# A fused attention and mixture-of-experts kernel: expert weights fetched in 256 KB pieces, the row-turning steps interleaved, and the first output bank fixed

## The chip, the cores and the metric

The kernel runs on one core of a Trainium2 chip. The metric is device time in microseconds for one execution, the median of several runs. A core has five engines that each run their own instruction list in order and wait for one another through semaphores: TensorE (PE, matrix products, with its weight loads shown apart as PEld), VectorE (DVE), ScalarE (ACT), GpSimd (POOL) and SyncE (SP, which here only issues transfers). POOL issues the indirect transfers (gathers and scatter-adds of rows), SP all others. The transfers run on 16 DMA engines that all queues share.

## What is computed

Windowed attention over 8 batches, 8 heads, 576 positions and 64 channels gives 4608 rows of 512 channels. A gate picks two of eight experts for each row, and each expert is two products with a ReLU between:

```python
logits = x @ w_gate
noise_scale = np.log1p(np.exp(x @ w_noise))
noisy_logits = logits + noise_scale * noise
top2 = np.argpartition(-noisy_logits, 2, axis=1)[:, :2]
...
for e in range(E):                      # 8 experts, w1[e] 512x1024, w2[e] 1024x512
    for k in range(2):
        mask = top2[:, k] == e
        h = np.maximum(x[mask] @ w1[e], 0.0)
        out[mask] += top2_w[mask, k, None] * (h @ w2[e])
```

## The kernel before

Attention and routing take the first quarter of the time and are not touched. Then the experts run one after another, and each expert's rows in chunks (`work`, L644): three chunks for expert 0, and two, of 576 and of 640 rows, for each of experts 1 to 7. The loop at L1116 writes, for each chunk, first `up` (the first product) and then `down` (the second). In both, matrix products are yielded step by step, and `spread` (L77) puts side work between the steps: a part `(a, b, list)` gives its items evenly from share a to share b of the steps. This fixes where an instruction stands in its engine's list; when it runs is set by its waits.

Operands of the products are split in a high and a low part (an ACT copy to `fp32r`, then a DVE subtraction), and every product is three matmuls. `up` for experts 1 to 7 uses seven half-size block products instead of eight (`PRODUCT`, L53); so the rows' planes (`turn`) and the blocks of w1 (`split_w1`) are combined by sums and differences first.

What one chunk needs:

- **Rows.** POOL gathers 128 rows at a time into `xg` (L675); SP writes them to DRAM (`turn_out`, L687, tile `xs`) and reads them back in four transfers in another order (`turn_in`, L692, tile `xc`). All of this for the next chunk stands in the first 0.65 of the steps of `up`.
- **Turning.** `turn` (L719) makes from `xc` the planes of the next chunk, as side work of `down` from step 12.5 to 0.86 of the steps. For each of its five tiles of 128 rows (the last one of a 576-row chunk has 64) there are two items. Item `f` (L728) does two DVE transposes into `tq`, planes 0 to 3 (L737). Item `g` (L745) does, in this order: ACT copy of planes 1 to 3 to `xh` (L749); DVE difference for planes 4 and 5 (L750); DVE low part of planes 1 to 3 (L751); two DVE differences for planes 6 and 7 (L752, L753); ACT copy of planes 4 to 7 (L755); DVE low part of those (L756). `tq` has one buffer, taken anew for each tile.
- **Weights.** One staging tile `ws` of 2 MB holds w1 or w2 of an expert in turn. `load_w1` of the next expert stands at the start of the first chunk's `down`, `load_w2` of the next expert behind the last chunk's `down`, each as a single transfer of 2 MB. `split_w2` stands in 0.55 to 1.0 of the first chunk's `up` and reads `ws` in slices in the order 0, 4, 1, 5, 2, 6, 3, 7; `split_w1` stands in the second chunk's `up` and `down` (its last items up to 0.9 of `down`).
- **Banks.** PSUM has three banks for `up` sums (`ps_z`), one `ps_v` and one `ps_y`. `down` writes its tiles in turn to `ps_d0`, `ps_d1` and `ps_y` (`ring("d")`, L818, a counter that runs on over all chunks), and each is evicted by ACT L997, or for a half tile by ACT L999 and DVE L1000 and L1001. The first product of the next `up` goes to `ps_v`, the second to `ps_y` (`start`, L875).

`down` of experts 1 to 7 begins with 4 steps of its first tile, then two products left over from `up` (`late`) with more steps of tiles 0 and 1 between, and only then the last two slices of w2 (slices 3 and 7, in the entry `(0, 6, 8)` of L967).

Of the kernel before, what the change touches and what calls it, by code (L numbers as in the profile page):

```python
# [8 lines left out]
F32 = mybir.dt.float32  # L9
# [9 lines left out]
N, DM, E, F = 4608, 512, 8, 1024  # L19
# [3 lines left out]
KD, KF = DM // 128, F // 128  # L23
# [7 lines left out]
HALF = WIDE // 2  # L31
# [28 lines left out]
def tiles(e, c):  # L60
    n = chunks(e)[c]
    return [(q, min(128, n - q * 128)) for q in range(-(-n // 128))]
# [25 lines left out]
def tile_kernel(ctx, tc, qT, kT, vx, vT, wgx, noise, w1, w2, out):  # L88
# [123 lines left out]
    def load_w1(e, ks=slice(0, KD), fs=slice(0, F)):  # L212
        if e < E:
            nc.sync.dma_start(w1s[:, ks, fs], w1[e][:, ks, fs])

    def load_w2(e, ks=slice(0, KF)):
        if e < E:
            nc.sync.dma_start(w2s[:, ks], w2[e][:, ks])
# [56 lines left out]
    def split_w2():  # L275
        return lag([(w2s[:, f], W2["h"][:, f], W2["l"][:, f]) for f in (0, 4, 1, 5, 2, 6, 3, 7)])
# [442 lines left out]
    def turn(e, c):  # L719
        if e == 0:  # L720
            return turn_first(c)
        todo = {}

        def begin():
            todo["h"] = XH[e, c] = exa.tile([128, 7, 2, HALF], F32R, name="xh")
            todo["l"] = XL[e, c] = exa.tile([128, 7, 2, HALF], F32R, name="xl")

        def f(q, m):  # L728
            if q == 0:
                begin()  # L730
            w = m // 2
            t = todo[q] = EXB["p"].tile([128, 4 * HALF], F32, name="tq", bufs=1)
            v = t[:, :16 * w].rearrange("p (s x) -> p s x", s=8)
            for h in range(2):
                d = v[:, 2 - 2 * h:4 - 2 * h].rearrange("p s (k x) -> p (s k) x", k=2).rearrange("p k (t c) -> p t k c", c=32)
                a = h * (CHUNKS[c] // 64) + 2 * q
                nc.vector.transpose(d, XC[e, c][:, a:a + w // 32].rearrange("p t (k c) -> p t k c", c=32))  # L737

        def parts(q, m, s0, s1):
            w = m // 2  # L740
            a = todo[q][:, s0 * 2 * w:s1 * 2 * w].rearrange("p (a x) -> p a x", x=w)
            return (a, *(x.rearrange("p a k x -> p (a k) x")[:, 2 * s0 - 2:2 * s1 - 2, q * 64:q * 64 + w]
                         for x in (todo["h"], todo["l"])))

        def g(q, m):  # L745
            w = m // 2
            v = todo[q][:, :16 * w].rearrange("p (s x) -> p s x", s=8)
            a, h, l = parts(q, m, 1, 4)
            nc.scalar.activation(h, a, AF.Copy)  # L749
            nc.vector.tensor_tensor(v[:, 4:6], v[:, 0:1].to_broadcast([128, 2, 2 * w]), v[:, 1:3], op=OP.subtract)  # L750
            nc.vector.tensor_tensor(l, a, h.bitcast(F32), op=OP.subtract)  # L751
            nc.vector.tensor_tensor(v[:, 6], v[:, 1], v[:, 5], op=OP.subtract)  # L752
            nc.vector.tensor_tensor(v[:, 7], v[:, 3], v[:, 6], op=OP.subtract)  # L753
            a2, h2, l2 = parts(q, m, 4, 8)
            nc.scalar.activation(h2, a2, AF.Copy)  # L755
            nc.vector.tensor_tensor(l2, a2, h2.bitcast(F32), op=OP.subtract)  # L756
        return [lambda q=q, m=m, x=x: x(q, m) for q, m in tiles(e, c) for x in (f, g)]

    pair = []

# [13 lines left out]
    EXB, BANKS = {}, {}  # L774
# [41 lines left out]
    late, turns = [], {"z": 0, "d": 0}  # L816
# [141 lines left out]
    def down(e, c):  # L958
        if e == 0:
            yield from down_first(c)  # L960
            return
        wt = GW[e, c]
        hb = HH.pop((e, c))
        w2h, w2l = W2["h"], W2["l"]
        order = (0, 4, 1, 5, 2, 6, 3, 7)
        size = dict(tiles(e, c))
        steps = [(0, 0, 4), None, (0, 4, 6), (1, 0, 2), None, (1, 2, 6), (0, 6, 8), (1, 6, 8)]  # L967
        steps += [(q, 0, 8) for q in size if q > 1]
        P_ = {}
        for s in steps:  # L970
            if not s:
                yield from late.pop(0)
                continue
            q, i0, i1 = s
            m = size[q]
            if i0 == 0:
                P_[q] = ring("d")
            p = P_[q]
            for i in range(i0, i1):
                f = order[i]  # L980
                a, b = dict(start=(i == 0), stop=False), dict(start=False, stop=(i == KF - 1))
                if m == 128:
                    h, l = (hb[:, x, f, q * 128:q * 128 + 128] for x in range(2))
                    nc.tensor.matmul(p, lhsT=h, rhs=w2h[:, f, :], **a)  # L984
                    nc.tensor.matmul(p, lhsT=h, rhs=w2l[:, f, :], start=False, stop=False)  # L985
                    nc.tensor.matmul(p, lhsT=l, rhs=w2h[:, f, :], **b)  # L986
                else:
                    t = hb[:, 0, f, q * 128:q * 128 + 2 * m]
                    nc.tensor.matmul(p, lhsT=t, rhs=w2h[:, f, :], **a)
                    nc.tensor.matmul(p, lhsT=t, rhs=w2l[:, f, :], **b)  # L990
                if i < KF - 1:
                    yield
            if i1 < KF:
                continue
            y = exa.tile([128, XW], F32, name="xg", bufs=XB)[:, :DM]
            if m == 128:
                nc.scalar.activation(y, p, AF.Copy, scale=wt[:, q:q + 1])  # L997
            else:
                nc.scalar.activation(y[:m], p[m:2 * m], AF.Copy)  # L999
                nc.vector.tensor_tensor(y[:m], y[:m], p[:m], op=OP.add)  # L1000
                nc.vector.tensor_scalar(y[:m], y[:m], wt[:m, q:q + 1], None, op0=OP.mult)  # L1001
            add_rows(e, c, q, m, y)
            yield
# [46 lines left out]
    for j in range(NT + 3):  # L1050
# [18 lines left out]
        if W1G // 2 - 4 <= j < W1G // 2 + 4:  # L1069
            k = j - W1G // 2 + 4  # L1070
# [45 lines left out]
    for n, (e, c) in enumerate(work):  # L1116
        nxt = work[n + 1] if n + 1 < len(work) else None
        last = c == len(chunks(e)) - 1
        side, parts = [], []
        if n == 0:  # L1120
            for w in split_w2():
                side += [lambda: (drain(3), drain_slots(1))] * 2 + [w]

            def catch_up():
                while (0, 1, 2) not in XG:
                    drain(1)
                    drain_slots(1)
        elif n == 1:
            pending.append(count())
            side += [lambda: (drain(6), drain_slots(1))] * 12  # L1130
            side += [settle, lambda: drain_slots(10 ** 6), lambda: [x() for x in first_list(2)], lambda: None]
        elif c == 0:
            parts.append((0.55, 1.0, split_w2()))
        if nxt and n:
            rows_of = gather(*nxt)
            if n < 2:
                side += rows_of + [lambda: None] * 2
            else:
                parts.append((0.0, 0.65, rows_of))
        if last and nxt:  # L1140
            nextw = split_w1(e == 0)
            parts += ([(0.55, 0.75, nextw[0]), (0.8, 1.0, nextw[1])] if e else
                      [(a, b, nextw[q]) for q, a, b in ((0, 0.02, 0.12), (1, 0.14, 0.3), (2, 0.33, 0.5), (4, 0.34, 0.5),
                                                       (3, 0.55, 0.75), (5, 0.56, 0.75), (6, 0.8, 1.0))])
        parts.append((0.0, 1.0, side))
        if n == 0:
            parts.append((0.0, 0.8, [zero_out] * ZUP))
        spread(up(e, c) if n else up00, 52 if e else KF * KD - (0 if n else len(taken)), *parts)
        side = turn(*nxt) if nxt else []
        total = KF * len(tiles(e, c)) + (4 if e else 0)  # L1150
        free = 12.5 / total
        if e == 0:
            parts = [(0.7, 1.0, side) if nxt[0] == 0 else (0.05, 0.85, side)]
            if last:
                parts.append((0.0, 0.4, nextw[7]))
        else:
            if c == 0:
                load_w1(e + 1)
            parts = [(free, 0.86, side)]
            if last and nxt:  # L1160
                parts.append((free, 0.9, nextw[2] + nextw[3]))
        if n == 1:
            load_w1(1)
            parts.append((0.0, 0.6, list(other_lists())))
        if n == 0:
            parts.append((0.0, 1.0, [lambda: (drain(3), drain_slots(1))] * 29))
            parts.append((0.68, 0.69, [catch_up]))
            parts.append((0.0, 0.6, [zero_out] * len(blank)))
        spread(down(e, c), total, *parts)
        if last:  # L1170
            load_w2(e + 1)
    ex.close()


# [115 lines left out]
```

## Time and profile before

| what | value |
|---|---|
| median of 3 runs | 1079.51 us (1073.28, 1079.51, 1079.69) |
| span of the profiled execution, first to last instruction | 1070.0 us |
| PE busy | 994.8 us, 93% of the span |
| DVE, ACT, POOL busy | 715.2, 521.8, 338.5 us |
| matmuls of `up` for experts 1 to 7, chunk of 320 columns, one | 310 ns modelled duration |
| matmuls of `down`, 512 columns, one | 390 ns modelled duration |
| `up` of experts 1 to 7 begins | 330 us, then about every 52 us |

The span is 9.5 us under the median and 3.3 us under the fastest run. In the profile a matmul's start is exact enough to see when PE was held up; its end is modelled, and matmuls overlap, so PE's busy share says little about pace. Rows of the list of waits name the waiting engine and line, then who released it, then total us, how many times, and the longest one. In the order of time a number in brackets behind a row is the engine's idle time before it and who ended it.

### The profile page before, as it was taken

Reading aid. Unit: us, or ns where it says so; the run is one execution under the profiler, and the core shown is the slowest. Engines: PE = TensorE matmul, PEld = TensorE weight load, DVE = VectorE, ACT = ScalarE, POOL = GpSimd, SP = SyncE. Lnnn points to the kernel's source line nnn. Section 1 sums busy time; section 2 is a strip of 40 time slices with the busy share of each in tenths; the row PEclk is TensorE's granted clock in tenths of the full one; section 3 lists DMA queues with packets and bytes.
Section 4 is the critical chain, followed back from the end, with each engine's and each line's share of the span. In section 5 each row is a group of like instructions: output and inputs, shape, how many; then the busy total and the mean of one; then the engine's idle time right before and its main releaser. Section 6 shows DMA issues by size and latency. Waiting matters only on the chain.

```text
span 1070.0 us, 22034 instructions
## 1 busy us (share of the span) xinstructions
PE 994.8 (93%) x8433; PEld 882.8 (83%) x8433; DVE 715.2 (67%) x1804; ACT 521.8 (49%) x1305; POOL 338.5 (32%) x465
## 2 busy tenths in 40 slices
PE   8787878779999999999999999999999999999995
PEld 8676767668788898889898889898889897989894
DVE  5688888684276667666776677677666866686630
ACT  4885666432244444544463446354644554454430
POOL 5436636333223141413132213222322323132202
PEclk9998998989999999999999999999999999999998
DMA  9987887874357653665377626762765385537303
GB/s 340 364 259 230 252 257 239 273 230 113 49 131 193 168 115 65 188 169 119 61 204 162 149 25 206 162 145 30 230 136 140 43 244 124 125 69 209 45 2 51
DMA packets 107235, 168.94 MB, mean 158 GB/s; under 512 B 13360, under 2 KB 57648, under 8 KB 105328
## 3 DMA queue, kind: packets, MB, share of 16 engines
q1 hardware_dynamic: 89968, 126.96, 38.7%
q0 software_dynamic: 17152, 40.48, 20.8%
q8 instruction: 68, 1.11, 0.4%
q14 instruction: 47, 0.39, 0.1%
HBM read 110.08 MB, written 57.32 MB: 156 GB/s over the span
## 4 chain that ended last, share of the span: by engine, by line
PE 42%; DVE 30%; ACT 8%; DMA 8%; issue 8%; POOL 1%; SPq 1%; DVEq 0%; POOLq 0%; ACTq 0%
PE ps_z L841 4%; PE ps_z L843 4%; PE ps_z L842 4%; DVE tq L737 4%; DVE WL L234 3%; ACT xh L755 3%; DVE xl L756 3%; DMA xc<-xs 3%; DVE xl L751 2%; PE ps_d L985 2%; PE ps_d L984 2%; PE ps_d L986 2%; DVE ws L264 2%; DVE pt L358 2%; DMA xs<-xg 2%
## 5 line engine op out<-in xcount | busy, mean ns | idle before, releaser
L919 POOL DMA_INDIRECT out_dram<-xg,los x70 | 111.1, 1587 | 423.7 <-ACT xg L997 364.5
L853 ACT ACTIVATE hb<-tq 128x288 fp32r<-128x288 f32 (+1 forms) x168 | 77.1, 459 | 144.4 <-DVE tq L872 138.7
L841 PE MATMUL ps_z<-xh,WH 128*128 128x288 f32 (+1 forms) x448 | 137.4, 307 | 0.9
L842 PE MATMUL ps_z<-xl,WH 128*128 128x288 f32 (+1 forms) x448 | 135.6, 303 | 0.0
L843 PE MATMUL ps_z<-xh,WL 128*128 128x288 f32 (+1 forms) x448 | 135.6, 303 | 0.0
L872 DVE TENSOR_TENSOR tq<-ps_z,tq 128x288 f32<-128x288 f32 (+1 forms) x168 | 79.3, 472 | 81.8 <-PE ps_z L843 76.4
L985 PE MATMUL ps_d<-w2l,hb 128*128 128x512 f32 x328 | 127.9, 390 | 0.0
L984 PE MATMUL ps_d<-w2h,hb 128*128 128x512 f32 x328 | 127.8, 390 | 0.0
L986 PE MATMUL ps_d<-w2h,hb 128*128 128x512 f32 x328 | 127.7, 389 | 0.0
L857 DVE SCALAR_TENSOR_TENSOR hb<-tq,hb 128x320 fp32r<-128x320 f32 (+2 forms) x168 | 75.5, 449 | 37.6 <-ACT hb L853 34.2
L675 POOL DMA_INDIRECT xg<-xrows,lxs x70 | 71.1, 1016 | 83.7 <-DMA xs<-xg 39.0
L841 PEld LDWEIGHTS ps_z<-xh,WH 128*128 128x128 f32 x448 | 84.8, 189 | 5.2 <-DVE tq L872 3.8
L842 PEld LDWEIGHTS ps_z<-xl,WH 128*128 128x128 f32 x448 | 84.8, 189 | 1.1
L755 ACT ACTIVATE xh<-tq 128x512 fp32r<-128x512 f32 (+1 forms) x70 | 42.7, 611 | 87.9 <-DVE tq L753 87.9
L843 PEld LDWEIGHTS ps_z<-xh,WL 128*128 128x128 f32 x448 | 84.7, 189 | 0.0
L756 DVE TENSOR_TENSOR xl<-tq,xh 128x512 fp32r<-128x512 f32 (+1 forms) x70 | 46.6, 666 | 47.4 <-ACT xh L755 47.4
L395 ACT ACTIVATE x<-ps_o,r 128x80 f32<-128x80 f32 x288 | 67.0, 348 | 15.2 <-DVE r L387 15.0
L986 PEld LDWEIGHTS ps_d<-w2h,hb 128*128 128x128 f32 x328 | 61.6, 188 | 13.0
L984 PEld LDWEIGHTS ps_d<-w2h,hb 128*128 128x128 f32 x328 | 61.6, 188 | 12.1
L985 PEld LDWEIGHTS ps_d<-w2l,hb 128*128 128x128 f32 x328 | 61.6, 188 | 11.8
L234 DVE TENSOR_TENSOR WL<-ws,WH 128x512 fp32r<-128x512 f32 x112 | 66.5, 613 | 3.8 <-ACT WH L242 3.4
L749 ACT ACTIVATE xh<-tq 128x384 fp32r<-128x384 f32 (+1 forms) x70 | 35.6, 508 | 68.0 <-DVE tq L737 68.0
(248 smaller groups left out, 2562.5 us busy)
## 6 DMA issues: line engine op xcount, KB each, us to landing
ws<-in_w_dram SPq DMA_DIRECT2D x14, 2048.0 KB
xs<-xg SPq DMA_DIRECT2D x63, 256.0 KB
vw<-in_vx_dram SPq DMA_DIRECT2D x36, 272.0 KB
out_dram<-zero SPq DMA_DIRECT2D x38, 256.0 KB
qc<-in_qT_dram SPq DMA_DIRECT2D x36, 256.0 KB
KW<-in_kT_dram SPq DMA_DIRECT2D x36, 256.0 KB
vt<-in_vT_dram SPq DMA_DIRECT2D x36, 256.0 KB
xrows<-x SPq DMA_DIRECT2D x36, 256.0 KB
```

What stands on the lines that cost most here:

```text
L234: eng.tensor_tensor(l, x, h.bitcast(F32), op=OP.subtract)
L756: nc.vector.tensor_tensor(l2, a2, h2.bitcast(F32), op=OP.subtract)
L841: nc.tensor.matmul(p[:, :n], lhsT=WH[:, a, k, w], rhs=xh[:, b, k, :n], start=first and k == 0, stop=False, **free)
L842: nc.tensor.matmul(p[:, :n], lhsT=WH[:, a, k, w], rhs=xl[:, b, k, :n], start=False, stop=False, **free)
L843: nc.tensor.matmul(p[:, :n], lhsT=WL[:, a, k, w], rhs=xh[:, b, k, :n], start=False, stop=(k == 1), **free)
L853: nc.scalar.activation(hh[:, f, a:b], src, AF.Relu)
L857: nc.vector.scalar_tensor_tensor(hl[:, f, a:m], src[:, :m - a], 0.0, hh[:, f, a:m].bitcast(F32), op0=OP.max, op1=OP.subtract)
L872: nc.vector.tensor_tensor(t, a[:, :n], t, op=OP.add)
L919: s = nc.gpsimd.indirect_dma_start(out=out[:(2 + seen.get((e, c), NT)) * 128], out_offset=bass.IndirectOffsetOnAxis(ap=LT[e, c][1][q][:m], ...
L984: nc.tensor.matmul(p, lhsT=h, rhs=w2h[:, f, :], **a)
L985: nc.tensor.matmul(p, lhsT=h, rhs=w2l[:, f, :], start=False, stop=False)
L986: nc.tensor.matmul(p, lhsT=l, rhs=w2h[:, f, :], **b)
```

## The change

Three edits, all for experts 1 to 7.

1. `turn` takes one `tq` for a whole chunk, and its items change: the second half of `g` (copy and low part of planes 4 to 7) becomes an item `last`, and the list is f0, then for each tile g, the next tile's f, and `last`: 15 items where there were 10, in the same stretch of `down`.
2. `down` sets the bank counter, so that its tiles always go to `ps_d0`, `ps_d1`, `ps_y`, `ps_d0`, `ps_d1`.
3. `load_w2(e)` moves from behind the last `down` of expert e-1 into 0.05 to 0.55 of the first `up` of expert e, as eight transfers of one slice in the order in which `split_w2` reads them. `load_w1(e + 1)` becomes eight transfers in 0.1 to 0.6 of the first chunk's `down`.

```diff
         def f(q, m):
             if q == 0:
                 begin()
+                todo["t"] = EXB["p"].tile([128, 4 * HALF], F32, name="tq", bufs=1)
             w = m // 2
-            t = todo[q] = EXB["p"].tile([128, 4 * HALF], F32, name="tq", bufs=1)
+            t = todo["t"]
...
             nc.vector.tensor_tensor(v[:, 7], v[:, 3], v[:, 6], op=OP.subtract)
+
+        def last(q, m):
             a2, h2, l2 = parts(q, m, 4, 8)
             nc.scalar.activation(h2, a2, AF.Copy)
             nc.vector.tensor_tensor(l2, a2, h2.bitcast(F32), op=OP.subtract)
-        return [lambda q=q, m=m, x=x: x(q, m) for q, m in tiles(e, c) for x in (f, g)]
+        todo_list = tiles(e, c)
+        out_ = [lambda: f(*todo_list[0])]
+        for i, (q, m) in enumerate(todo_list):
+            out_.append(lambda q=q, m=m: g(q, m))
+            if i + 1 < len(todo_list):
+                out_.append(lambda i=i: f(*todo_list[i + 1]))
+            out_.append(lambda q=q, m=m: last(q, m))
+        return out_
...
         P_ = {}
+        turns["d"] = 2
         for s in steps:
...
         elif c == 0:
+            parts.append((0.05, 0.55, [lambda f=f: load_w2(e, slice(f, f + 1)) for f in (0, 4, 1, 5, 2, 6, 3, 7)]))
             parts.append((0.55, 1.0, split_w2()))
...
         else:
+            parts = [(free, 0.86, side)]
             if c == 0:
-                load_w1(e + 1)
-            parts = [(free, 0.86, side)]
+                parts.append((0.1, 0.6, [lambda k=k, x=x: load_w1(e + 1, slice(k, k + 1), slice(x * F // 2, x * F // 2 + F // 2))
+                                         for x in range(2) for k in range(KD)]))
...
         spread(down(e, c), total, *parts)
-        if last:
-            load_w2(e + 1)
```

The line numbers behind the edits grow by up to 11 (L737 becomes L738, L756 becomes L759, L841 becomes L851, L986 becomes L997).

DVE's list in `down` of a first chunk, from the first tile of `turn` to the transposes of the second. Before:

```order
L737 STREAM_TRANSPOSE tq<-xc 128x2x4x32 x2
L750 TENSOR_TENSOR tq<-tq 128x256
L751 TENSOR_TENSOR xl<-tq,xh 128x6x64
L752 TENSOR_TENSOR tq<-tq 128x128
L753 TENSOR_TENSOR tq<-tq 128x128
L756 TENSOR_TENSOR xl<-tq,xh 128x8x64
L737 STREAM_TRANSPOSE tq<-xc 128x2x4x32 x2
```

And of the change, the same place:

```order
L738 STREAM_TRANSPOSE tq<-xc 128x2x4x32 x2
L751 TENSOR_TENSOR tq<-tq 128x256
L752 TENSOR_TENSOR xl<-tq,xh 128x6x64
L753 TENSOR_TENSOR tq<-tq 128x128
L754 TENSOR_TENSOR tq<-tq 128x128
L738 STREAM_TRANSPOSE tq<-xc 128x2x4x32 x2
L759 TENSOR_TENSOR xl<-tq,xh 128x8x64
```

The second tile's transposes now stand between the differences and the low part of planes 4 to 7, which waits for an ACT copy.

PE's list at the border from the second chunk of expert 1 to the first of expert 2: the end of the last tile of `down`, then the first two products of `up`. Before:

```order
L985 MATMUL ps_y_3972<-w2l,hb 128x512
L986 MATMUL ps_y_3972<-w2h,hb 128x512
L841 MATMUL ps_v_3971<-xh,WH 128x288
L842 MATMUL ps_v_3971<-xl,WH 128x288
L843 MATMUL ps_v_3971<-xh,WL 128x288
L841 MATMUL ps_v_3971<-xh,WH 128x288
L842 MATMUL ps_v_3971<-xl,WH 128x288
L843 MATMUL ps_v_3971<-xh,WL 128x288
L841 MATMUL ps_y_3972<-xh,WH 128x288
```

And of the change, at the same border:

```order
L996 MATMUL ps_d_3967<-w2l,hb 128x512
L997 MATMUL ps_d_3967<-w2h,hb 128x512
L851 MATMUL ps_v_3971<-xh,WH 128x288
L852 MATMUL ps_v_3971<-xl,WH 128x288
L853 MATMUL ps_v_3971<-xh,WL 128x288
L851 MATMUL ps_v_3971<-xh,WH 128x288
L852 MATMUL ps_v_3971<-xl,WH 128x288
L853 MATMUL ps_v_3971<-xh,WL 128x288
L851 MATMUL ps_y_3972<-xh,WH 128x288
```

Where the last tile of `down` stood in `ps_y` (4 of the 13 borders with an `up` of experts 1 to 7 behind a `down` of the same), it now stands in `ps_d1`, at every border.

SP's list over one first chunk's `up` and the start of its `down` (`ws` is the staging tile; the transfers `xs` and `xc` in front are those of the chunk before). Before:

```order
L687 DMA xs<-xg 64x512
L692 DMA xc<-xs 32x18x128 x4
L218 DMA ws<-in_w_dram 128x4096
L687 DMA xs<-xg 128x512 x5
L692 DMA xc<-xs 32x20x128 x4
L214 DMA ws<-in_w_dram 128x4096
```

And of the change:

```order
L692 DMA xc<-xs 32x18x128 x4
L218 DMA ws<-in_w_dram 128x512 x2
L687 DMA xs<-xg 128x512 x2
L218 DMA ws<-in_w_dram 128x512
L687 DMA xs<-xg 128x512 x2
L218 DMA ws<-in_w_dram 128x512 x3
L687 DMA xs<-xg 128x512
L218 DMA ws<-in_w_dram 128x512
L692 DMA xc<-xs 32x20x128
L218 DMA ws<-in_w_dram 128x512
L692 DMA xc<-xs 32x20x128 x3
L214 DMA ws<-in_w_dram 128x512 x8
```

Two pieces of w2 stand ahead of the first write of rows, the seventh behind the fifth write, and the eighth behind the first read in the new order.

## Rows read from the trace of the kernel before

**Rows 1.** Waits of PE from 320 us on: total us, times, longest.
```profile
PE ps_y L841 <- DVE xg L1000: 3.2, 2, 1.6
PE ps_y L841 <- ACT xg L997: 3.1, 2, 1.5
PE ps_v L841 <- ACT xh L749: 2.1, 1, 2.1
PE ps_v L842 <- DVE xl L751: 1.8, 8, 0.3
```

**Rows 2.** The same of PE's weight loads.
```profile
PEld ps_v L841 <- ACT xh L749: 5.7, 9, 2.5
PEld ps_v L842 <- DVE xl L751: 4.0, 9, 0.5
PEld ps_y L842 <- DVE xl L756: 2.2, 6, 0.5
```

**Rows 3.** PE in order of time, first `up` of expert 2: start us, us, instruction.
```profile
434.76 0.40 PE L841 MATMUL ps_v<-xh,WH 128*128 128x288 f32 x1
435.41 0.40 PE L842 MATMUL ps_v<-xl,WH 128*128 128x288 f32 x1 [0.25 <-DVE xl L751]
```

**Rows 4.** PE by stretches: us, PE busy (matmuls), granted clock, DMA share, GB/s.
```profile
438.10:441.50 3.40, 3.40 (x16) 0.50 0.83 224
441.50:444.90 3.40, 3.40 (x27) 1.00 0.95 365
...
591.70:595.10 3.40, 3.27 (x12) 0.50 0.20 22
...
332.30:335.70 3.40, 3.37 (x13) 0.50 0.57 77
```

**Rows 5.** The page, part 5: busy us, mean ns, idle us before and its releaser.
```profile
L756 DVE TENSOR_TENSOR xl<-tq,xh 128x512 fp32r<-128x512 f32 (+1 forms) x70 | 46.6, 666 | 47.4 <-ACT xh L755 47.4
```

**Rows 6.** DVE in order of time, first `down` of expert 3.
```profile
569.29 0.46 DVE L857 SCALAR_TENSOR_TENSOR hb<-ps_z,hb 128x288 fp32r<-128x288 f32 x1 [2.47 <-ACT hb L853]
571.78 0.77 DVE L737 STREAM_TRANSPOSE tq<-xc 128x256 f32<-128x256 f32 x2 [2.04 <-DMA xc<-xs]
...
590.42 0.69 DVE L756 TENSOR_TENSOR xl<-tq,xh 128x512 fp32r<-128x512 f32 x1 [0.70 <-ACT xh L755]
```

**Rows 7.** All engines in order of time, the border behind that `down`.
```profile
588.66 0.41 PE L841 MATMUL ps_v<-xh,WH 128*128 128x320 f32 x1
...
590.42 0.59 ACT L999 ACTIVATE xg<-ps_y 64x512 f32<-64x512 f32 x1
```

**Rows 8.** The same at the border from expert 3 to expert 4.
```profile
645.24 0.40 PE L841 MATMUL ps_v<-xh,WH 128*128 128x288 f32 x1
...
645.48 0.35 DVE L751 TENSOR_TENSOR xl<-tq,xh 128x192 fp32r<-128x192 f32 x1
```

**Rows 9.** SP's transfers in order of time, expert 3, both chunks.
```profile
543.09 0.35 SPq L218 DMA_DIRECT2D ws<-in_w_dram  x1
553.46 7.38 SPq L687 DMA_DIRECT2D xs<-xg  x5
562.66 1.97 SPq L692 DMA_DIRECT2D xc<-xs  x4
...
597.66 8.53 SPq L687 DMA_DIRECT2D xs<-xg  x5
```

**Rows 10.** POOL's first gather of each of these chunks.
```profile
544.79 1.02 POOL L675 DMA_INDIRECT xg<-xrows,lxs  x1 [0.30 <-issue]
...
594.31 1.02 POOL L675 DMA_INDIRECT xg<-xrows,lxs  x1 [0.30 <-issue]
```

**Rows 11.** The chain that ended last, 562 to 573 us: start us, us, what.
```profile
564.12 7.44 DMA xc<-xs
```

**Rows 12.** ACT and PE in order of time: last split of w2, first use of its last slices.
```profile
560.55 0.62 ACT L242 ACTIVATE w2h<-ws 128x512 fp32r<-128x512 f32 x1
...
571.38 0.39 PE L984 MATMUL ps_d<-w2h,hb 128*128 128x512 f32 x1
```

More of the change, by code (lines that the diff above doesn't have):

```diff
@@ L740, in parts @@
             w = m // 2
-            a = todo[q][:, s0 * 2 * w:s1 * 2 * w].rearrange("p (a x) -> p a x", x=w)
+            a = todo["t"][:, s0 * 2 * w:s1 * 2 * w].rearrange("p (a x) -> p a x", x=w)
             return (a, *(x.rearrange("p a k x -> p (a k) x")[:, 2 * s0 - 2:2 * s1 - 2, q * 64:q * 64 + w]
@@ L746, in g @@
             w = m // 2
-            v = todo[q][:, :16 * w].rearrange("p (s x) -> p s x", s=8)
+            v = todo["t"][:, :16 * w].rearrange("p (s x) -> p s x", s=8)
             a, h, l = parts(q, m, 1, 4)
```

## Prediction

> **What bounds the kernel now.** I read the page first: PE is busy nearly throughout the expert stage, so the change can win only where PE is held up there. Then I asked for the waits of PE alone, from 320 us on, where experts 1 to 7 run. The reader is to see two kinds [rows 1]. Four waits of about 1.6 us, 3.2 + 3.1 = 6.3 us in all, stand before `ps_y` L841: the second product of an `up` waits until the last tile of the `down` before it is evicted from the same bank (L997, or L999 to L1001). And PE waits for `turn`: once 2.1 us, and eight times up to 0.3 us, for the planes of `xh` and `xl` that its first product reads. The weight loads, which run a step ahead, show the same waits larger, because a modelled matmul end covers part of a hold-up [rows 2]. The order of time shows one: 0.65 us between two matmul starts [rows 3], where 27 of these matmuls take 3.4 us, so 0.13 us each [rows 4].
>
> Next I looked at the granted clock. Three times in this stage it falls to half (1.2 instead of 2.4 GHz) for 3.4 us [rows 4], and each time PE had just waited 1.5 us or more: behind the wait at the first `up` of expert 1, and behind two of the four `ps_y` waits. The other two had no fall behind them.
>
> Last, the order of time of DVE and ACT before a border says why the waits are there. In the first `down` of expert 3, DVE goes through the five tiles of `turn` without a break from 571.78 to 591.11 us, 3.87 us a tile, and in every full tile it stands idle 0.70 us before L756, for the ACT copy of planes 4 to 7 [rows 6]; in the whole kernel that idle time is 47.4 us [rows 5]. PE's next `up` begins at 588.66, while the turning is in its last tile, and the eviction of the last bank (ACT L999, at 590.42) stands behind the turning's copies [rows 7]. At the border to expert 4 it is the same: PE begins at 645.24, and the low part that it needs is made from 645.48 to 645.83 [rows 8].
>
> **The bank order.** The tile in `ps_y` becomes the third of five, evicted in mid `down`, and the last tile lies in `ps_d1`, which no product of `up` writes. The four waits go: 6.3 us [rows 1]. Nothing is added. The next user of `ps_d0` or `ps_d1` is a whole `up` later, and within a `down` a bank comes back after three tiles, as before. Alone this would win a little less, since at these borders the second product would then wait for L756, which ends 0.7 us ahead of the half tile's eviction; with the turning shortened it doesn't.
>
> **The turning.** The same instructions run, in another order: the next tile's two transposes (0.77 us together [rows 6]) now stand where DVE waited 0.70 us for ACT. I count the wait as gone: 2.8 us less before the last tile's L751. At the border of rows 8 that low part ends at 643.0 instead of 645.8, 2.2 us ahead of PE. At the border of rows 7 the last tile's L751 ends at 589.2 now, and 586.4 then, 2.3 us ahead. So these waits go whole. Their size: from below 2.1 + 1.8 = 3.9 us [rows 1]; from above 5.7 + 4.0 + 2.2 = 11.9 us [rows 2]. Start to start, the hold-up of rows 3 is 0.65 - 0.13 = 0.52 us; nine such (the count in rows 2) are 4.7 us; with the 2.2 us for L756 and the 2.1 us at expert 1 that is 9.0. I take 8, leaving 1 us for borders that are not quite cleared. A copy of planes 4 to 7 now stands a little later on ACT, for the last tile behind the eviction of the fourth; the product that reads those planes is PE's second, so about 0.9 us are in hand there beside the 2 us above.
>
> **The clock.** A fall costs (27 - 16) matmuls of 0.13 us, 1.4 us, and at most half of 3.4, 1.7 us [rows 4]. Three cost 4.2 to 5.1 us, if all go because no wait of 1.5 us is left, and nothing is won if other falls come in their place. I take 3.5.
>
> **The weights.** By itself I cost this edit at nothing. What it moves: the first gather of expert 3's second chunk is issued at 544.79, and its first write to `xs` at 553.46, 8.7 us later, while the 2 MB issued at 543.09 are on their way; in the other `up`, without such a load, it is 594.31 to 597.66, 3.4 us [rows 9, 10]. With two pieces, a quarter of the bytes, ahead of the first write, I estimate 3.4 + 5.3 / 4 = 4.7 us, so writes and reads come 4 us earlier, and `xc`, which lands at 571.56 now [rows 11], before 568. DVE reaches its first transposes at 569.75 and waits 2.04 us for `xc` [rows 6]; that wait goes too. But with the shorter turning those 2 us only add to the 2.3 us in hand. SP issues 13 loads as 104, 91 more of about 0.35 us [rows 9], 2.8 us a load on an engine that mostly waits. w1 has slack: its first reader stands in the second `up`, a whole `down` later. w2 is closer: its eighth piece stands on SP behind the first read into `xc`, which waits for all five writes. ACT reaches the split of that slice at 560.55, and PE first needs the last slices at 571.38 [rows 12]. ACT's copy is 0.62 us; DVE's low part and the results of `up` queued behind both I put at 3.7 us. So PE waits only if the piece lands after 567.1. I expect its issue near 559 and its landing before 563.
>
> A page speaks against small transfers. The Trainium skill, "DMA: Bandwidth & Descriptors", section "Anatomy of one DMA — SWDGE (gpsimd) path", gives each transfer about 2.0 us of fixed cost and the bytes at 436 GB/s on top; by that a 256 KB piece is 2.6 us (an estimate, from a path that SP does not use), and eight in a row are 20.8 us, against 6.8 us for one of 2 MB. Started at 543.1 they would end at 563.9, still ahead of 567.1, so the sum by the page is the same. The rows give no price of such a piece in this stage.
>
> **The sum.** 6.3 + 8 + 3.5 = 17.8 us off the span of 1070.0: 1052.2. The median of the runs is 9.5 us over the profiled span, so I forecast 1062. With the bounds of the terms (10.2 to 23.3 us) that is 1056 to 1069.
>
> **Rivals.**
>
> *Banks only (14 in 100).* The ACT copies of the turning wait for PE through the evictions between them, and DVE waits at L756's new place as long as before. For it: the last copy does stand behind the fourth tile's eviction. Against it: DVE trails PE now, so those evictions are due when ACT comes to them. It leaves 6.3 us and two falls of the clock (2.8) less some 2 us for L756 at those borders: 7 us off, 1072.
>
> *Given back (10 in 100).* PE comes earlier to other waits: DVE still has w1's splits to do when `up` begins, and `ps_z` waits for its additions. Against it: DVE's own stretch shrinks by as much as PE comes earlier, and those splits move up with it. At half the gain that is 9 us off: 1071.
>
> *The last piece of w2 comes late (12 in 100), the other side.* The place is the SP queue: the eighth piece is issued behind the first read into `xc`, at worst at 562.7 as now [rows 9], and shares the DMA engines with the reads, which take 7.44 us [rows 11]; landing at 570.4, it holds PE for 570.4 - 567.1 = 3.3 us in each of seven experts, 23 us. That ends at 1062 + 23 = 1085. It decides from a landing after 567.1; at 569.6 (2.5 us an expert) the gain is eaten up, and over 1% slower needs 571.1. Against it: the first writes should come 4 us earlier, not later.
>
> *The pieces are not spread (no chance of its own).* SP is held by waits alone, not by PE's steps, so several pieces may leave together. The time is that of the forecast, because the edit is costed at nothing.
>
> **How the numbers follow.** The forecast has 64 in 100, with its own range of 1056 to 1069. The range for 8 in 10 goes up to the two rivals with a small gain and a little below the forecast's low end: 1055 to 1075. About 1% is what a measurement of this kernel can tell from no change; faster by that means under 1068.7. The forecast lies there but for its edge: 0.64 with a little of the two small-gain cases. Slower by over 1% needs the late piece at its worst, 0.05. The rest, 0.31, is within 1%.
>
> **What would show it.** Right: no wait of PE on L997, L999 or L1000 (new L1008 to L1011) before `ps_y`; the idle time before the low part of planes 4 to 7 (L759) near zero instead of 47.4 us; PE's waits on L751 and L756 (new L752, L759) under 2 us in all; no half-clock stretch from 330 us to the end of the matmuls; the first write of rows in a first chunk's `up` about 5 us behind its gather. Wrong: a PE wait of several us at the entry `(0, 6, 8)` behind w2's split (then the late piece), or ACT waiting for `ws` before L242; DVE idle before L759 as before (banks only); longer waits at `ps_z` (given back); or a span that shrinks without the median following.

## The result: 1% slower, and the profile after

The change takes 1088.07 us (median of 4 runs, 1085.58 to 1095.72), the kernel before 1077.54 us in the same comparison: a ratio of 1.010 with a 95% interval of 1.006 to 1.014. The forecast was 1062, with a range of 1055 to 1075. The profiled execution took 1085.58 us with a span of 1083.9, 13.9 us over the span before. Those two numbers lie 1.7 us apart: the 9.5 us that the forecast put between a span and a median were mostly the spread of the runs. One execution among the experiments below, of the kernel with turning and banks alone, took 1112.84 us at a mean granted clock of 0.84 where the others had 0.975 to 0.979; that kernel's time is the median of the other three.

The waits of PE from 320 us on, to be read against [rows 1]. Columns: total us, times, longest.

```profile
PE ps_z L851 <- DVE tq L882: 16.7, 7, 3.9
PE ps_v L851 <- ACT tq L877: 10.7, 8, 2.5
```

Every wait of [rows 1] is gone: none on the eviction of a `down` tile, none on the turning. In their place stand 27.4 us of waits: 10.7 us inside `up` for evictions of `ps_v`, and 16.7 us for the additions on DVE that empty `ps_z`, all but 0.2 us of it before the products left over from `up` that stand early in `down`. The other engines' waits in the same stretch say where these come from:

```profile
ACT w2h L242 <- DMA ws<-in_w_dram: 40.7, 21, 3.4
DVE w2l L234 <- ACT w2h L242: 37.5, 20, 3.3
```

ACT waits 21 times, two to four times in each of seven experts, for a piece of w2 (some 32 of the 40.7 us for the seventh and the eighth), and DVE, which makes the low part, waits behind it. The order of time of all engines shows one such place, at the first product left over from the first `up` of expert 3:

```profile
568.74 0.63 ACT L242 ACTIVATE w2h<-ws 128x512 fp32r<-128x512 f32 x1 [2.73 <-DMA ws<-in_w_dram]
569.27 0.39 ACT L877 ACTIVATE tq<-ps_v 128x288 f32<-128x288 f32 x1
569.40 0.69 DVE L234 TENSOR_TENSOR w2l<-ws,w2h 128x512 fp32r<-128x512 f32 x1 [2.56 <-ACT w2h L242]
570.01 0.45 DVE L882 TENSOR_TENSOR tq<-ps_z,tq 128x288 f32<-128x288 f32 x1
...
570.52 0.61 PE L851 MATMUL ps_z<-xh,WH 128*128 128x288 f32 x1 [2.91 <-DVE tq L882]
```

The reader is to see one late piece hold two lists. On ACT the split waits 2.73 us for it, and the eviction of `ps_v` stands behind the split. On DVE the low part waits 2.56 us for the split, and the addition that empties `ps_z` stands behind the low part; it starts at 570.01, when the eviction has been over for 0.35 us, so here DVE's own list held it last. PE needs the `ps_z` bank. PE is not waiting for w2.

Why the piece is late is in the chain of what ended last, followed in order of time (start us, us, what):

```profile
542.21 2.91 DMA ws<-in_w_dram
545.20 4.97 DMA xg<-xrows,lxs
550.19 3.97 DMA xs<-xg
554.20 0.70 issue
554.90 6.64 DMA xg<-xrows,lxs
561.56 2.19 DMA xs<-xg
563.83 0.33 SPq L692
564.20 4.52 DMA ws<-in_w_dram
568.74 0.64 ACT w2h L242
```

The first pieces leave at 542.21, and the eighth at 564.20. Between them SP stands in its list at the fifth write of rows (561.56), which waits for the fifth gather. POOL can issue that one only at 554.90, when a buffer of `xg` is written out, and it takes 6.64 us to land. The gather shares the DMA engines with three pieces that SP sent off just before:

```profile
554.25 1.42 SPq L218 DMA_DIRECT2D ws<-in_w_dram  x3
561.56 0.33 SPq L687 DMA_DIRECT2D xs<-xg  x1
561.93 0.43 SPq L218 DMA_DIRECT2D ws<-in_w_dram  x1
563.83 0.33 SPq L692 DMA_DIRECT2D xc<-xs  x1
564.20 0.51 SPq L218 DMA_DIRECT2D ws<-in_w_dram  x1
```

The clock falls too. Two of the stretches at half clock, as in [rows 4] (us, PE busy and matmuls, granted clock, DMA share, GB/s), and the one behind them at nearly full clock:

```profile
461.00:464.40 3.40, 1.56 (x6) 0.50 1.20 196
464.40:467.80 3.40, 3.40 (x10) 0.50 1.07 290
467.80:471.20 3.40, 3.40 (x19) 0.99 0.91 336
```

From 330 us to the end of the matmuls there are eight stretches of 3.4 us at half clock, in six experts; before there were three. The expert stage, from the start of the first matmul of expert 1's `up` to the start of the last matmul, took 726.2 us before and takes 743.5 now.

### The profile page after: what moved, and what is told of

Read it like the earlier page. It is cut to its first block, busy times and chain, and to the rows that moved or that the text cites. A ratio compares the mean times of both kernels' runs of the same rounds, so it can differ in the third digit from the quotient of the medians.

```text
span 1083.9 us, 22236 instructions
## 1 busy us (share of the span) xinstructions
PE 992.7 (92%) x8433; PEld 884.9 (82%) x8433; DVE 712.1 (66%) x1804; ACT 524.2 (48%) x1305; POOL 337.2 (31%) x465
## 4 chain that ended last, share of the span: by engine, by line
PE 42%; DVE 21%; DMA 17%; issue 12%; ACT 4%; POOL 3%; SPq 1%; POOLq 0%; ACTq 0%; DVEq 0%
DMA xg<-xrows,lxs 6%; PE ps_d L995 6%; PE ps_d L996 6%; PE ps_d L997 6%; DMA xs<-xg 5%; DMA ws<-in_w_dram 4%; PE ps_z L851 3%; DVE WL L234 3%; PE ps_z L853 3%; PE ps_z L852 3%; DVE pt L358 2%; DVE xl L759 2%; PE ps_o L376 2%; DVE t L335 1%; DVE mx L340 1%
## 5 line engine op out<-in xcount | busy, mean ns | idle before, releaser
L995 PE MATMUL ps_d<-w2h,hb 128*128 128x512 f32 x392 | 156.4, 399 | 0.0
L851 PE MATMUL ps_z<-xh,WH 128*128 128x288 f32 (+1 forms) x448 | 139.7, 312 | 17.6 <-DVE tq L882 16.7
L996 PE MATMUL ps_d<-w2l,hb 128*128 128x512 f32 x392 | 155.7, 397 | 0.0
L997 PE MATMUL ps_d<-w2h,hb 128*128 128x512 f32 x392 | 155.0, 395 | 0.0
L851 PEld LDWEIGHTS ps_z<-xh,WH 128*128 128x128 f32 x448 | 85.3, 190 | 24.8 <-DVE tq L882 23.2
L997 PEld LDWEIGHTS ps_d<-w2h,hb 128*128 128x128 f32 x392 | 75.3, 192 | 16.4
L995 PEld LDWEIGHTS ps_d<-w2h,hb 128*128 128x128 f32 x392 | 75.9, 194 | 14.8
L996 PEld LDWEIGHTS ps_d<-w2l,hb 128*128 128x128 f32 x392 | 75.8, 193 | 14.3
L851 PE MATMUL ps_v<-xh,WH 128*128 128x288 f32 (+1 forms) x196 | 59.9, 306 | 10.7 <-ACT tq L877 10.7
L234 DVE TENSOR_TENSOR w2l<-ws,w2h 128x512 fp32r<-128x512 f32 x64 | 43.8, 686 | 37.6 <-ACT w2h L242 37.5
L376 PE MATMUL ps_o<-vw,pt 64*64 64x85 f32 x2176 | 54.5, 249 | 13.2 <-issue 6.5
```

What stands on the lines that cost most here:

```text
L234: eng.tensor_tensor(l, x, h.bitcast(F32), op=OP.subtract)
L376: nc.tensor.matmul(PO[j][u * 64:u * 64 + 64, a, g * 2 + x, :], lhsT=pt[pa, w, u * 2 + g, x * 64:x * 64 + 64], rhs=v[pa, (i + w) % 2, :, u, ...
L851: nc.tensor.matmul(p[:, :n], lhsT=WH[:, a, k, w], rhs=xh[:, b, k, :n], start=first and k == 0, stop=False, **free)
```

## The experiments

The theory after the result: the turning and the banks win what was forecast, or more, and w2's pieces lose more than that, because the last of them are queued on SP behind the writes of rows. The rivals: the new order of the turning costs the time itself; small pieces are slow wherever they stand; PE waits for w2 itself. Each run below was compared with the kernel before on the same chip (medians there 1076 to 1078 us).

**One edit of the change undone: w2 again in one transfer.** (`x1_no_w2`)

```diff
-            parts.append((0.05, 0.55, [lambda f=f: load_w2(e, slice(f, f + 1)) for f in (0, 4, 1, 5, 2, 6, 3, 7)]))
...
         spread(down(e, c), total, *parts)
+        if last:
+            load_w2(e + 1)
```

> The change with one edit undone: w2 is again fetched as one transfer of 2 MB behind the last down; the turning, the bank order and w1 in pieces stay. Theory (the late pieces of w2, queued on SP behind the writes of rows, hold ACT at the split of w2 and with it the evictions that free ps_v and ps_z): no wait of PE on L877 or L882 over 1 us, border waits gone as in the change, 1058 to 1066 us. Rival (the reordered turning and the fixed bank order cost the time themselves): stays at 1083 to 1092. Rival (w1 in pieces is to blame): stays above 1080 too.

Measured: 1050.17 us, ratio 0.975 (0.972 to 0.978). The list of PE's waits from 320 us on is empty, there is no half-clock stretch there, and the expert stage takes 702.7 us. So the whole loss, 38 us, belongs to the one edit that the prediction had costed at nothing, and the rest wins 27 us, more than the 17.8 us of the forecast; the time lies under the range expected here for the same reason.

**That edit alone on the kernel before.** (`x2_only_w2`)

```diff
+            parts.append((0.05, 0.55, [lambda f=f: load_w2(e, slice(f, f + 1)) for f in (0, 4, 1, 5, 2, 6, 3, 7)]))
...
-        if last:
-            load_w2(e + 1)
```

> The kernel before with one edit alone: w2 in eight pieces in 0.05 to 0.55 of the first up. Theory of the late pieces: the waits of PE on the ACT and DVE evictions inside the first up appear here as in the change, about 25 us, on top of the border waits that are kept, some of which shrink because PE is late: 1088 to 1108 us. Rival (turning or banks cost the time): near 1078, within 5 us.

Measured: 1107.31 us, ratio 1.029 (1.025 to 1.034). The waits of PE are those of the change and of the kernel before together (of the latter, the two waits on L1000 shrink from 3.2 to 1.3 us):

```profile
PE ps_v L841 <- ACT tq L867: 12.7, 7, 3.4
PE ps_z L841 <- DVE tq L872: 11.0, 8, 2.4
PE ps_y L841 <- ACT xg L997: 3.1, 2, 1.5
```

Eight half-clock stretches lie in the expert stage here, against three before. The first two rows are 23.7 us; five more falls at 1.4 to 1.7 us [rows 4] make 7 to 8.5 us. Together that is 31 to 32 us, and 30 were measured.

**The same eight pieces, all ahead of the first write on SP.** (`x3_w2_front`)

```diff
-            parts.append((0.05, 0.55, [lambda f=f: load_w2(e, slice(f, f + 1)) for f in (0, 4, 1, 5, 2, 6, 3, 7)]))
+            parts.append((0.0, 0.1, [lambda f=f: load_w2(e, slice(f, f + 1)) for f in (0, 4, 1, 5, 2, 6, 3, 7)]))
```

> The change with the eight pieces of w2 in 0.0 to 0.1 of the first up, so that all stand on SP ahead of the first write of rows; same pieces, same order among themselves. Theory (place in SP's list): the ACT waits for ws go, 1058 to 1067 us. Rival (256 KB pieces are slow in themselves, wherever they stand): ACT still waits for ws and the time stays above 1080. Rival (bandwidth: the rows' transfers are the ones that come late): xc lands as late as in the kernel before, with no loss because the turning is shorter: also near 1062.

Measured: 1050.82 us, ratio 0.975 (0.973 to 0.978), as with one transfer, and under the expected range like it. Expert 3 on SP:

```profile
535.34 5.24 SPq L218 DMA_DIRECT2D ws<-in_w_dram  x8
547.52 8.38 SPq L687 DMA_DIRECT2D xs<-xg  x5
557.62 1.97 SPq L692 DMA_DIRECT2D xc<-xs  x4
```

All eight leave within 5.24 us, and the first write then comes 12.2 us behind the first piece, where the change has 8.0 (542.21 to 550.19). So small pieces cost the kernel nothing here; the place in SP's list decides. The rival that the rows come late holds as well: DVE's waits for `xc`, in the kernel before and in this one, are

```profile
DVE tq L737 <- DMA xc<-xs: 7.4, 5, 2.2
DVE tq L738 <- DMA xc<-xs: 20.9, 7, 4.7
```

and PE still waits only 1.1 us in all. Rows that come later cost nothing once the turning is short.

**The seventh and eighth piece ahead of the fifth write.** (`x8_two_ahead`)

```diff
-            parts.append((0.05, 0.55, [lambda f=f: load_w2(e, slice(f, f + 1)) for f in (0, 4, 1, 5, 2, 6, 3, 7)]))
+            parts.append((0.05, 0.44, [lambda f=f: load_w2(e, slice(f, f + 1)) for f in (0, 4, 1, 5, 2, 6, 3, 7)]))
```

> The change with the pieces of w2 in 0.05 to 0.44 of the first up: on SP still two ahead of the first write and six between or behind the first four writes, but now the seventh and eighth stand ahead of the fifth write, and none among the reads into xc. Theory (the last two wait on SP for the fifth gather, its write and the first read): ACT's longest waits for ws, 2.2 and 2.7 us at the last two slices, go, PE's waits inside the first up fall from 27 us to under 8, 1054 to 1064 us. Rival (pieces queued behind any write are late): most of the loss stays, above 1075.

Measured: 1067.01 us, ratio 0.990 (0.987 to 0.992), a little over the expected range; eight of nine executions took 1063 to 1068 us, and the profiled one 1054. Its waits:

```profile
PE ps_v L851 <- ACT tq L877: 9.1, 6, 2.6
ACT w2h L242 <- DMA ws<-in_w_dram: 7.6, 10, 1.6
```

ACT's waits for `ws` fall from 40.7 to 7.6 us, and PE's from 27.4 to 9.1: those at `ps_z` go, 16.7 us, and those at `ps_v` stay, 9.1 of 10.7. No half-clock stretch is left in the expert stage of this execution, and that stage takes 712.0 us, 9.3 us more than with w2 in one transfer. By the medians 21 of the 38 us hung on those two pieces. The other waits stand at the fourth to the sixth slice, whose pieces are still behind writes.

**Once more, for its profile.** (`x8_again`, the same kernel)

> The kernel of x8_two_ahead once more, for its profile: its profiled execution was 1054 us and its eight others 1063 to 1068. If the waits of PE that are left bring falls of the clock in most executions and none in that one, a second profile shows half-clock stretches from 330 us on and 10 us more, 1063 to 1068 us; if it is the transfers, longer waits for ws at full clock.

One execution, 1058.32 us: PE waits 8.6 us for the same eviction, ACT 8.0 us for `ws`, and one half-clock stretch lies in the expert stage, at 860 us; the other profile had none. The two executions differ by 4 us, but their expert stages by only 1.1 (713.1 against 712.0). Neither what was expected of the clock nor what was expected of the transfers is shown: neither profile is one of the executions over 1063, and why these were slower is open.

**The banks alone, on the kernel before.** (`x4_only_banks`)

```diff
         P_ = {}
+        turns["d"] = 2
```

> The kernel before with the bank counter set at each down and nothing else. By the prediction's first term: the four waits before ps_y go, but the second product then waits about 0.5 us for the turning at these borders, and two falls of the clock go: 5 to 9 us under the kernel before, 1069 to 1073. If the rival holds that bank order costs time elsewhere: 1078 or more.

Measured: 1073.96 us, ratio 0.996 (0.994 to 0.999): 4 us, less than expected.

```profile
PE ps_v L842 <- DVE xl L751: 2.2, 10, 0.2
PE ps_v L841 <- ACT xh L749: 2.1, 1, 2.1
PE ps_y L842 <- DVE xl L756: 1.9, 6, 0.3
PE ps_y L841 <- ACT xh L755: 1.0, 5, 0.2
```

The last two rows in the kernel before:

```profile
PE ps_y L842 <- DVE xl L756: 0.6, 2, 0.3
PE ps_y L841 <- ACT xh L755: 0.2, 1, 0.2
```

The waits on L997 and L1000 are gone, but the waits on the turning at `ps_y`, L755 and L756, grow in their place. That fits an eviction that was late because it stood behind the turning in ACT's and DVE's lists; the next experiment tests it. The profile has one half-clock stretch in the expert stage, at 334 us, where the kernel before had three, so two falls went as expected. At 1.4 to 1.7 us each they make up most of the 3.7 us by which this stage is shorter (722.5 against 726.2): the waits themselves were mostly exchanged.

**The turning alone, on the kernel before.** (`x6_only_turn`: the first edit of the change and nothing else)

```diff
+                todo["t"] = EXB["p"].tile([128, 4 * HALF], F32, name="tq", bufs=1)
...
-            t = todo[q] = EXB["p"].tile([128, 4 * HALF], F32, name="tq", bufs=1)
+            t = todo["t"]
...
-        return [lambda q=q, m=m, x=x: x(q, m) for q, m in tiles(e, c) for x in (f, g)]
+        out_ = [lambda: f(*todo_list[0])]
+        for i, (q, m) in enumerate(todo_list):
+            out_.append(lambda q=q, m=m: g(q, m))
+            if i + 1 < len(todo_list):
+                out_.append(lambda i=i: f(*todo_list[i + 1]))
+            out_.append(lambda q=q, m=m: last(q, m))
+        return out_
```

> The kernel before with the turning alone interleaved. With both edits the span fell by some 23 us in the expert stage, with the bank order alone by 4. Additive: the four ps_y waits stay (1.5 us each, the eviction now a little earlier), the others go: 1055 to 1062 us. Rival (the two hang together: the eviction of the last bank was late only because of the turning in front of it, so the turning alone removes these waits too): 1048 to 1053.

Measured: 1049.62 us, ratio 0.975 (0.970 to 0.980).

```profile
PE ps_y L851 <- DVE xg L1010: 1.3, 2, 0.6
PE ps_v L851 <- ACT tq L877: 0.8, 2, 0.5
```

Of the four waits on the last bank, 6.3 us [rows 1], 1.3 us are left although the bank order is the old one. The rival held: the turning alone takes the whole gain, within what the measurement tells apart. (In the profiles its expert stage is 3.0 us longer than with the banks, 705.9 against 702.9; but the profiled execution is the slowest of its four, 1052.80 us against 1049.3 to 1049.7.)

**Turning and banks, no weight edit.** (`x5_turn_banks`)

```diff
+            if c == 0:
+                load_w1(e + 1)
             parts = [(free, 0.86, side)]
-            if c == 0:
-                parts.append((0.1, 0.6, [lambda k=k, x=x: load_w1(e + 1, slice(k, k + 1), slice(x * F // 2, x * F // 2 + F // 2))
-                                         for x in range(2) for k in range(KD)]))
```

(and w2 in one transfer, as in the first experiment)

> The change without both weight edits: w1 and w2 each one transfer as before; the turning and the bank order stay. If w1 in pieces is worth nothing, as the prediction had it: as with w2 alone undone, 1047 to 1054 us. Rival (w1 in pieces relieves the reads into xc): 3 us or more above that.

Measured: 1049.33 us, ratio 0.975 (0.968 to 0.982). The same as with w1 in pieces.

**w1 in pieces alone, on the kernel before.** (`x7_only_w1`)

```diff
+            parts = [(free, 0.86, side)]
             if c == 0:
-                load_w1(e + 1)
-            parts = [(free, 0.86, side)]
+                parts.append((0.1, 0.6, [lambda k=k, x=x: load_w1(e + 1, slice(k, k + 1), slice(x * F // 2, x * F // 2 + F // 2))
+                                         for x in range(2) for k in range(KD)]))
```

> The kernel before with w1 alone in eight pieces. Costed at nothing in the prediction: within 4 us of the kernel before. If the pieces behind the reads into xc let those land sooner, the 2 us that DVE waits for xc in each first down shrink and the borders gain: up to 6 us under it. If the pieces slow the reads: over it.

Measured: 1076.64 us, ratio 1.000 (0.997 to 1.002). The border waits of [rows 1] stand as they were, 3.2 and 3.1 us on the banks; this profile has five half-clock stretches in the expert stage, one at each of these four waits and one at the wait at expert 1, where the kernel before had three. So w1 is worth nothing, as forecast.

**The change with the split of w2 on GpSimd.** (`x9_split_on_pool`)

```diff
     def split_w2():
+        def on_pool(f):
+            nc.gpsimd.tensor_copy(W2["h"][:, f], w2s[:, f])
+            nc.gpsimd.tensor_tensor(W2["l"][:, f], w2s[:, f], W2["h"][:, f].bitcast(F32), op=OP.subtract)
+        if "z" in BANKS and late_split[0]:
+            return [lambda f=f: on_pool(f) for f in (0, 4, 1, 5, 2, 6, 3, 7)]
...
+    late_split = [False]
...
+            late_split[0] = True
             parts.append((0.55, 1.0, split_w2()))
```

> The change as it is, its pieces of w2 as late as there, but the split of w2 for experts 1 to 7 (copy and low part) on GpSimd instead of ScalarE and VectorE. Theory (PE is not held for w2 itself, which it first reads some 30 us after the up begins, but for the evictions that stand on ScalarE behind the waiting split): ScalarE has no wait for ws, PE's waits inside the first up go, 1047 to 1060 us. Rival (w2 arrives too late for PE's first use of the last slices): PE waits at the first use of slices 3 and 7 in down, above 1075 us.

Measured: 1063.24 us, ratio 0.987 (0.980 to 0.994), 25 us under the change, but 3 over the range that the theory gave. In expert 3 the eighth piece leaves 21.3 us behind the first, as in the change (22.0), and PE waits elsewhere:

```profile
540.46 0.88 SPq L218 DMA_DIRECT2D ws<-in_w_dram  x2
...
561.75 0.51 SPq L218 DMA_DIRECT2D ws<-in_w_dram  x1
```

```profile
PE ps_d L1003 <- POOL w2l L278: 9.9, 16, 1.1
PE ps_z L858 <- DVE tq L889: 1.5, 7, 0.3
```

There are no waits for `ws` on ACT, none of PE on `ps_v`, and no half-clock stretch in the expert stage. The 9.9 us that are left come from GpSimd's pace, as its order of time shows for the last slices of expert 3:

```profile
567.34 0.61 POOL L277 CAST w2h<-ws 128x512 fp32r<-128x512 f32 x1
568.03 1.31 POOL L278 TENSOR_TENSOR w2l<-ws,w2h 128x512 fp32r<-128x512 f32 x1
569.29 0.60 POOL L277 CAST w2h<-ws 128x512 fp32r<-128x512 f32 x1
569.98 1.30 POOL L278 TENSOR_TENSOR w2l<-ws,w2h 128x512 fp32r<-128x512 f32 x1
```

A slice takes 1.95 us there and it works without a break; it is not waiting for a piece. So pieces as late as those of the change do no harm to `up` when nothing that PE needs stands behind the instruction that waits for them. Together with the change's own list, which has no wait of PE for w2, that settles the rival: in the change PE was not held for w2.

Four versions lie near 1050 us: the turning alone, with the banks, with both and w1 in pieces, and the whole change with w2's pieces ahead of the writes. They can't be told apart by these runs.

## Why the prediction was wrong, step by step

**The weights: the step that failed.** The text said "So PE waits only if the piece lands after 567.1" and "I expect its issue near 559 and its landing before 563". Both halves were wrong, and the first weighs more.

The deadline was taken from PE's first use of the last slices of w2 [rows 12], with an allowance for the copy and what is queued behind it. But the lists that the copy and the low part stand in have nearer customers: behind the copy ACT evicts `ps_v`, behind the low part DVE empties `ps_z`, and PE needs these banks for the next products of `up` and for those left over from it. An instruction that waits is late for whoever waits for the ones behind it, not for its own reader alone. The prediction named the wait that the edit adds, and counted the results queued behind it as 3.7 us of work, but did not look up when PE needs those results. With the deadline put at the split's own slot on ACT, 560.55 in [rows 12], the last pieces had no slack at all; even a landing at 563 is 2.4 us behind it. That the rule failed, and not only the landing, shows when times are counted from PE's start of this `up`, before and now:

```profile
539.36 0.40 PE L841 MATMUL ps_v<-xh,WH 128*128 128x288 f32 x1
542.13 0.29 PE L851 MATMUL ps_v<-xh,WH 128*128 128x288 f32 x1
```

The deadline of the text, read off the kernel before, lay 27.7 us behind that start (567.1), and the eighth piece landed 26.6 us behind it (568.72). By the text's own rule it was in time and cost nothing; PE stood for 2.91 us all the same.

The landing: the first write was put at 4.7 us behind its gather, and it is 5.0 us (545.20 to 550.19). From there to the first read the text kept the old pace, 9.2 us [rows 9]. It is 13.6 us now (550.19 to 563.83). Of the 4.4 us more, 1.9 lie between the first write and the issue of the fifth gather, which waits for that write to land and free a buffer, and 2.5 between that gather and its write, while the fourth to sixth pieces are on the DMA engines with it. So the eighth piece left at 564.20 instead of about 559; the other 2.8 us of that are the later start of the `up`. Work that is moved out of the way of the first transfers was moved into the way of a later one, and the piece itself was queued behind that one.

The cost, worked out from the rows: 27.4 us of waits, and eight falls of the clock at 1.4 to 1.7 us each, 11 to 14 us; 39 to 41 us together, where the runs show 38 (1088.07 against 1050.17) and the two expert stages 40.8 (743.5 against 702.7).

The rival on the other side, "The last piece of w2 comes late", had the place: SP's queue, the eighth piece. Its size, 3.3 us in each of seven experts against 27.4 / 7 = 3.9, came near by luck. It let PE wait for w2 itself from a landing after 567.1 on, which would have cost nothing here, and it left out the clock. Its chance of 12 in 100 hung on the same deadline.

The other rule weighed there did not show either: eight pieces ahead of the writes give the same time as one transfer, 1050.82 against 1050.17 us. The Trainium skill, "DMA: Bandwidth & Descriptors", section "Anatomy of one DMA — SWDGE (gpsimd) path", fits 2.0 us plus the bytes at 436 GB/s to a transfer of a path that SP does not use; by that, an estimate, eight in a row are 20.8 us against 6.8 for one. The kernel time shows no such cost, and the times from issue to landing are others: 10.9 us in the median for a transfer of 2 MB (turning and banks), 5.4 for a piece (split on GpSimd), from these rows of the pages.

```profile
ws<-in_w_dram SPq DMA_DIRECT2D x14, 2048.0 KB, 10.9
ws<-in_w_dram SPq DMA_DIRECT2D x112, 256.0 KB, 5.4
```

**The turning: right, and too small.** It was put at 8 us between 3.9 and 11.9. DVE's idle time before the low part of planes 4 to 7 fell from 47.4 us [rows 5] to 11.0 in the kernel with turning and banks, and the waits at the borders went whole. The saving on a tile is more than the 0.70 us of [rows 6]: with w2 undone DVE goes through a tile in 2.84 us, where it took 3.87.

```profile
571.21 0.66 DVE L759 TENSOR_TENSOR xl<-tq,xh 128x512 fp32r<-128x512 f32 x1
...
574.05 0.66 DVE L759 TENSOR_TENSOR xl<-tq,xh 128x512 fp32r<-128x512 f32 x1
```

**The banks: right in mechanism, not a term of its own.** 6.3 us were counted for them and 8 for the turning beside them. Alone they win 4 us, most of it two falls of the clock, and the turning alone wins all. The eviction was late because of the turning in front of it, as the prediction itself read in [rows 7]; so these 6.3 us belonged to the turning, and adding them was right only for both edits together.

**The clock: right for those two edits.** No half-clock stretch is left in the expert stage with the turning and the banks alone, so 4.2 to 5.1 us and not 3.5.

**The sum of these three** was 17.8 us, bounded at 23.3. The expert stage shows 23.3 us less (726.2 to 702.9 with turning and banks), at the upper bound, which takes the turning from the weight loads' rows [rows 2]: for it these were the better measure of a hold-up than the matmuls' own. That the two figures agree to a tenth is chance. The medians differ by 27.8, 4.5 us more than the stages. Of these, 2.2 us lie in which executions were profiled (1073.28 us before, 1047.69 with turning and banks: 25.6 apart). The kernel with w1 alone in pieces, in an execution of 1078.66 us, has the same border waits, five falls of the clock and a stage of 730.0 us; so a median execution of the kernel before may have more falls than its profile, which no run shows for that kernel itself.

**w1 in pieces: right.** It is worth nothing, alone or with the others.

Of what the text named as signs, the half that was to show it right came true at the borders, but not for the clock, nor for the idle time before the low part of planes 4 to 7: that is 20.6 us in the change, not near zero. Of the half that was to show it wrong, "ACT waiting for `ws` before L242" came true, and so did longer waits at `ps_z`, which the text had given to another rival; here they come from w2's low part on DVE.

## What to carry to other kernels

When a transfer is made later, its deadline is the slot of the instruction that waits for it, on that engine, plus whatever time passes until someone needs what stands behind that slot; the data's last reader may be far away and tell nothing. When transfers are spread in program order on one queue, each is as late as the slowest wait ahead of it in that queue: look for a gather or a buffer's release there before calling a transfer spread. And a wait that two edits would both remove is to be counted for one of them.

## What was not expected of the hardware

Short waits of PE can cost more than themselves, and do not always. In the change, 27.4 us of waits came with eight half-clock stretches, and the expert stage is 40.8 us longer than with w2 in one transfer. With the seventh and eighth piece moved, six waits of 0.5 to 2.6 us, 9.1 us in all, came with none, and the stage is 9.3 us longer. The kernel with the split on GpSimd had nine waits of 0.8 to 1.1 us in the expert stage and no such stretch. And the four waits on the last bank, 1.5 to 1.6 us each, came with two falls in the kernel before and with four in the kernel with w1 alone in pieces. So the length of a wait alone does not tell whether the clock falls; no run here shows what does.

A gather of 128 rows that has reached its write in about 3.4 us with no weights under way [rows 9, 10] took 5.0 us behind two pieces of 256 KB and 6.7 us beside three, all in expert 3. Over the seven first `up`s of the change the fifth gather takes 4.3 to 6.9 us to its write, and in the kernel before 3.6 to 5.2. That the pieces are what slows it is argued from these times; no run varies that alone.
